# Twenty idle products in place of 130 in the opening of an attention and feed-forward kernel

## The chip, the cores and the metric

The kernel runs on one core of a Trainium2 chip. The metric is the time of one execution on the device in microseconds, as the median of several runs. The profile is of one execution, taken by the hardware profiler; PE is TensorE, PEld its loads of weights, DVE is VectorE, ACT is ScalarE, POOL is GpSimd and SP is SyncE.

## What is computed

Sliding-window causal attention over 8 batches, 8 heads, 576 positions and 64 numbers a head, and a gated feed-forward network on its result:

```python
scores = scale * np.matmul(q, k.transpose(0, 1, 3, 2))
rel = pos[:, None] - pos[None, :]
mask = (rel >= 0) & (rel < 64)
...                                     # softmax over the masked scores
attn_out = np.matmul(attn, v)           # 8 x 8 x 576 x 64
x = attn_out.transpose(0, 2, 1, 3).reshape(4608, 512)
a = x @ w1                              # 512 x 1024
b = x @ w2                              # 512 x 1024
h = a * b @ w3                          # 1024 x 1024
return h @ w_out                        # 1024 x 512
```

Inputs and output are float32.

## The kernel before

Products are made in float16 with sums in float32. Since nothing lies between w3 and w_out, the kernel multiplies these two once, into a 1024 x 512 matrix `wc_sb`, and each token then needs only w1, w2 and `wc_sb`.

Every engine works through its instructions in the order in which the program lists them. The opening (L479 to L642) is an order written out by hand; from there a loop over slots interleaves the attention (18 steps of 256 positions) with the feed-forward part (9 groups of 512 tokens). The change lies in the opening.

What the opening does, for the names that matter here:

- `load_rows` (L419, SP queue) and `load_w3` (L430, POOL queue) bring rows of w3 in blocks of 128; `cast_rows` (L424) turns the blocks that came in float32 into float16. Blocks 0 and 1 come by the first way, blocks 2 and 3 by one transfer of the second way, into the tile that the profile calls `ab`.
- `fold_t(fc)` turns one block by eight products with the identity (L437), into a buffer of the four that are called `f_ps`, and an engine copies the result to `w3T` (L439).
- `load_wo` (L415) brings w_out in two halves of 256 columns, also into a tile called `ab`.
- `fold_mm(fc, c0, c1)` multiplies a turned block by columns of w_out (L444) and copies the result to `wc_sb` (L445).
- `load_qk` (L210) and `load_v` (L230) bring q, k and v; `transposes` (L220, VectorE) makes `kT` and `qT` from them; `scores` (L275) makes 64 small products for one step of attention, `weigh` (L284, L288, L245) the exponentials and the mask, `values` (L301, L307) and `norm` (L317 to L320) the result.
- `ffn_ab` (L367) and `ffn_o` (L383) are the feed-forward products; `store` (L397) writes the output.
- `keep_busy(n)` (L465 to L469) multiplies the identity by itself n times into one buffer of `f_ps` that nothing reads.

TensorE's order in the opening is: eight transposes of block 0, the products of `keep_busy`, sixteen transposes of blocks 2 and 3, the scores of step 0, eight transposes of block 1, and then the folding products of blocks 2, 3, 1 and 0 for the first 256 columns. POOL issues, in this order, the loads of k and q of batch 0, of w3's blocks 2 and 3, makes the band of the mask, and issues the loads of w_out's first and second half, of w3's blocks 4 and 5 and of v.

## Time and profile before

| | |
|---|---|
| median of three runs | 258.71 us (258.62 to 259.79) |
| the profiled execution: its own time | 257.93 us |
| its span | 256.1 us |
| TensorE busy | 245.0 us (96%) |
| VectorE, ScalarE, GpSimd busy | 146.4, 118.9, 114.9 us |
| idle products (L469) | 130, from 5.80 us on |
| first folding product (L444) | 18.46 us |

Times in the profile count from the start of the span; the execution's own time is longer by 1.8 us. In a row of the timeline stand the start, the time from the first start to the last end of the instructions that were merged, the engine, the line and the operation, what is written and read, how many, and in brackets the idle time before and what ended it. In a row of one line's instructions stand the shortest, the median and the longest duration of one in ns, and the first and the last start. A row of the chain has a start, a length and what filled it.

### The profile page before, as it was taken

The page shows a single profiled execution, that of the slowest core. Times are in us where ns is not written, and L with a number is a line of the kernel's source. Part 1 is how long each engine was busy: PE and PEld are TensorE (multiplying, and loading weights), DVE is VectorE, ACT ScalarE, POOL GpSimd, SP SyncE. Part 2 cuts the span into 40 slices and gives each one's busy share as a digit, 9 for nine tenths or more (in the row PEclk, how much of TensorE's full clock was granted, in tenths as well). Part 3 has the DMA queues.
Part 4 walks back from the last instruction along what each step waited for, and adds up shares of the span by engine and source line. Part 5 has one row for each costly group of instructions (what it writes and reads, how often), then busy time and mean ns, then how long its engine had stood idle before and what let it go on. Part 6 is the DMA issues. An engine that isn't in the chain of part 4 may idle for free.

```text
span 256.1 us, 8262 instructions
## 1 busy us (share of the span) xinstructions
PE 245.0 (96%) x3612; PEld 129.6 (51%) x3612; DVE 146.4 (57%) x217; ACT 118.9 (46%) x178; POOL 114.9 (45%) x153
## 2 busy tenths in 40 slices
PE   2989999999999999999999999999999999999991
PEld 2988654454445544445444444454444544444441
DVE  1173936778777646557764774675566345434420
ACT  2143672384475564454526444545465455233210
POOL 8873858599769855881097036003000303003000
PEclk9999999999999999999999999999999999999999
DMA  6999999999996999599079909401300220021022
GB/s 202 198 179 183 205 205 200 155 188 177 195 116 75 179 202 170 80 186 189 7 121 200 129 0 163 99 5 41 127 3 5 84 88 1 3 94 75 1 82 89
DMA packets 75657, 30.09 MB, mean 117 GB/s; under 512 B 62488, under 2 KB 70040, under 8 KB 75616
## 3 DMA queue, kind: packets, MB, share of 16 engines
q0 software_dynamic: 69712, 18.88, 74.0%
q1 hardware_dynamic: 5616, 10.44, 11.0%
q8 instruction: 29, 0.48, 0.8%
q10 hardware_dynamic: 288, 0.20, 0.2%
q14 instruction: 12, 0.10, 0.1%
HBM read 38.80 MB, written 9.44 MB: 188 GB/s over the span
## 4 chain that ended last, share of the span: by engine, by line
PE 90%; DMA 5%; POOL 1%; ACT 1%; issue 0%; DVE 0%; POOLq 0%
PE f_ps L367 49%; PE f_ps L383 24%; PE f_ps L444 6%; PE a_ps L275 4%; PE a_ps L307 4%; DMA ab<-in_moe_w_out_dram 3%; PE a_ps L301 2%; DMA k<-in_k_dram 2%; ACT pt L284 1%; PE f_ps L437 1%; POOL ab L430 0%; POOL band L247 0%; POOL band L245 0%; POOL band L254 0%; DVE t2k L390 0%
## 5 line engine op out<-in xcount | busy, mean ns | idle before, releaser
L367 PE MATMUL f_ps<-xT,w_sb 128*128 128x512 f16 x576 | 129.5, 379 | 0.0
L367 PEld LDWEIGHTS <-w_sb 128*128 128x128 f16 x576 | 54.7, 98 | 64.5 <-issue 0.8
L371 DVE TENSOR_TENSOR ab<-f_ps,a_sb 128x512 f16<-128x512 f32 x72 | 49.6, 690 | 41.0 <-PE f_ps L367 37.6
L383 PE MATMUL f_ps<-wc_sb,ab 128*128 128x512 f16 (+1 forms) x296 | 65.6, 374 | 0.0
L370 ACT COPY a_sb<-f_ps 128x512 f32<-128x512 f32 x72 | 42.2, 587 | 46.2 <-PE f_ps L367 46.2
L245 POOL TENSOR_SCALAR_AFFINE_SELECT pt<-pt 128x1024 f16<-128x1024 f16 x11 | 13.0, 1180 | 79.6 <-ACT pt L284 79.6
L383 PEld LDWEIGHTS <-ab 128*128 128x128 f16 x296 | 27.9, 98 | 31.0
L284 ACT ACTIVATE pt<-a_ps 128x1024 f16<-128x1024 f32 x36 | 36.3, 1026 | 15.1 <-PE a_ps L275 15.1
L320 DVE TENSOR_TENSOR xT<-a_ps,r 128x512 f16<-128x512 f32 x36 | 23.2, 687 | 25.1 <-ACT r L318 25.0
L230 POOL DMA_DIRECT2D v<-in_v_dram x40 | 34.6, 885 | 2.6 <-PE f_ps L367 1.1
L386 ACT COPY t2k<-f_ps 128x512 f32<-128x512 f32 (+1 forms) x19 | 10.9, 575 | 42.2 <-PE f_ps L383 42.2
L288 DVE TENSOR_TENSOR pt<-pt,band 128x1024 f16<-128x1024 f16 x25 | 17.3, 695 | 14.1 <-ACT pt L284 13.9
L210 POOL DMA_DIRECT2D k<-in_k_dram x32 | 20.2, 646 | 5.8 <-DMA v<-in_v_dram 3.5
L210 POOL DMA_DIRECT2D q<-in_q_dram x32 | 20.0, 637 | 4.3 <-DMA v<-in_v_dram 1.8
L220 DVE STREAM_TRANSPOSE kT<-k 128x576 int32<-128x576 int32 x16 | 14.9, 936 | 4.3 <-DMA k<-in_k_dram 4.3
L386 DVE COPY t2k<-f_ps 128x512 f32<-128x512 f32 x17 | 11.7, 688 | 9.1 <-PE f_ps L383 9.1
L220 DVE STREAM_TRANSPOSE qT<-q 128x576 int32<-128x576 int32 x16 | 14.8, 934 | 2.2 <-DMA q<-in_q_dram 2.2
L444 PE MATMUL f_ps<-ab,w3T 128*128 128x256 f16 (+1 forms) x96 | 14.6, 308 | 0.3 <-DMA ab<-in_moe_w_out_dram 0.3
L275 PEld LDWEIGHTS <-kT 32*128 32x128 f16 x1152 | 10.5, 92 | 7.8 <-issue 7.0
L307 PE MATMUL a_ps<-pt,v 128*32 128x64 f16 x1152 | 14.0, 193 | 0.0
L317 ACT ACTIVATE ln_s<-a_ps 128x512 f32<-128x512 f32 x18 | 10.8, 598 | 6.6 <-PE a_ps L301 6.5
L307 PEld LDWEIGHTS <-v 128*32 128x32 f16 x1152 | 13.5, 97 | 0.3
(47 smaller groups left out, 135.0 us busy)
## 6 DMA issues: line engine op xcount, KB each, us to landing
out_dram<-t2k SPq DMA_DIRECT2D x35, 256.0 KB, 4.4
k<-in_k_dram POOLq DMA_DIRECT2D x32, 144.0 KB, 7.6
q<-in_q_dram POOLq DMA_DIRECT2D x32, 144.0 KB, 6.6
v<-in_v_dram POOLq DMA_DIRECT2D x32, 128.0 KB, 5.9
w_sb<-in_moe_w_dram POOLq DMA_DIRECT2D x8, 256.0 KB, 9.8
w_sb<-in_moe_w_dram SPq DMA_DIRECT2D x2, 512.0 KB
ab<-in_moe_w_out_dram POOLq DMA_DIRECT2D x2, 512.0 KB, 9.1
xT<-in_moe_w_dram POOLq DMA_DIRECT2D x2, 512.0 KB, 12.5
```

What stands on the lines that cost most here:

```text
L210: nc.gpsimd.dma_start(out=t16_of(b, which)[32 * j:32 * j + 32].rearrange("p hh (i n) -> p (hh i) n", n=r * D), in_=src[b, 2 * j:2 * j + 2] ...
L220: nc.vector.transpose(dst[b][:, hh].rearrange("q t c -> q (t c)").bitcast(I32).rearrange("q (i p r) -> q i r p", p=32, r=r), t16s[which, b ...
L230: nc.gpsimd.dma_start(out=vh[lo:P, c], in_=v[b, :, s0:s0 + P - lo, :].rearrange("h s d -> s h d"))
L284: nc.scalar.activation(pt, held.pop(d).rearrange("k j (a n) -> k (j a) n", a=2), AF.Exp, bias=-SHIFT, scale=scale)
L307: nc.tensor.matmul(o_ps[jp][32 * h:32 * h + 32, 0, o0:o0 + 64], v16s[b % 3][:, max(0, t - 1), 4 * jp + h, x:D:2], pt[:, h, 64 * i:64 * i + ...
L320: nc.vector.tensor_tensor(xT[:, 2 * jp:2 * jp + 2, x0:x0 + W], o_ps[jp][:, 0].rearrange("p (x n) -> p x n", x=2), r[:, jp].unsqueeze(1).br ...
L367: nc.tensor.matmul(d[:, f * n:f * n + n], w[:, dc, (fc + f) * P:(fc + f + 1) * P], xT[:, dc, x0:x0 + n], start=(dc == 0), stop=(dc == 3), ...
L370: act_cp(a_sb[:, 0:nf * n], a_ps[:, 0:nf * n])
L371: nc.vector.tensor_tensor(ab[:, fc:fc + nf, lo:hi], b_ps[:, 0:nf * n].rearrange("p (f n) -> p f n", f=nf), a_sb[:, 0:nf * n].rearrange("p ...
L383: nc.tensor.matmul(o_ps[:, 0:c1 - c0], ab[:, fc, t * P:t * P + P], wc_sb[:, fc, c0:c1], start=(fc == 0), stop=(fc == 7))
L386: cp(o_sb[:, c0:c1], o_ps[:, 0:c1 - c0])
L444: nc.tensor.matmul(o_ps[:, c0:c1], w3Ts[fc][:, ec, :], wo16[:, ec, c0:c1], start=(ec == 0), stop=(ec == 7))
```

## The change

`keep_busy` is called with 20 in place of 130, at the same place. TensorE gets 110 products, with their loads of weights, fewer in the opening. No other instruction and no order is touched.

```diff
     make_band()
     cast_rows(1, 1, act_cp)
-    keep_busy(130)
+    keep_busy(20)
     load_wo(0, 256)
     fold_t(2, act_cp)
     fold_t(3, act_cp)
```

## The prediction

> **What bounds the kernel now.** I read the page first: the span, the busy times, the two rows of slices for TensorE, and the chain by engine.

> ```profile
> span 256.1 us, 8262 instructions
> PE 245.0 (96%) x3612; PEld 129.6 (51%) x3612; DVE 146.4 (57%) x217; ACT 118.9 (46%) x178; POOL 114.9 (45%) x153
> ...
> PE   2989999999999999999999999999999999999991
> ...
> PEclk9999999999999999999999999999999999999999
> ...
> PE 90%; DMA 5%; POOL 1%; ACT 1%; issue 0%; DVE 0%; POOLq 0%
> ```

> TensorE is busy for 96% of the span and carries 90% of the chain. So what matters is how early its real work begins and how fast it then runs. Second came the same engines cut into stretches, for the share in which TensorE has no slack at all.

> ```profile
> core 0: us, PE busy (x) PEld busy (x) DVE busy (x) ACT busy (x) POOL busy (x), PEclk, DMA share, GB/s
> 0.00:5.00 5.00, 0.03 (x1) 0.03 (x2) 0.52 (x3) 1.28 (x1) 4.03 (x12) 1.00 0.54 204
> 5.00:18.50 13.50, 12.64 (x227) 12.30 (x228) 5.71 (x7) 3.69 (x5) 11.12 (x17) 1.00 1.21 188
> 18.50:251.00 232.50, 232.35 (x3386) 117.27 (x3385) 139.89 (x208) 113.72 (x173) 99.78 (x125) 1.00 0.86 112
> 251.00:256.10 5.10, 0.00 (x0) 0.00 (x0) 0.29 (x1) 0.26 (x1) 0.00 (x0) 1.00 0.27 94
> ```

> From 18.50 to 251.00 us TensorE is busy for 232.35 of 232.50 us: 0.15 us of idle time in all. Whatever delays or slows it after 18.5 us reaches the end in full, because no later wait of its own can swallow it. Third: what it waits for, and the chain around 18 us.

> ```profile
> PE f_ps L437 <- DVE ab L424: 5.0, 1, 5.0
> PE a_ps L275 <- DVE kT L220: 0.5, 1, 0.5
> PE f_ps L444 <- DMA ab<-in_moe_w_out_dram: 0.3, 1, 0.3
> ```

> ```profile
> 10.21 8.21 DMA ab<-in_moe_w_out_dram
> 18.42 0.04 issue
> 18.46 6.27 PE f_ps L444 x56
> ```

> TensorE has only three waits. The last real gate is the first half of w_out, issued at 10.21 us and landed at 18.42, which releases the first folding products (L444) at 18.46. Before that gate TensorE's work is not on the chain, and the 130 idle products (L469) lie wholly there. Fourth, TensorE's timeline up to the gate:

> ```profile
> 4.97 1.03 PE L437 MATMUL f_ps<-ident,ab 128*128 128x128 f16 x8 [4.97 <-DVE ab L424]
> 5.80 9.67 PE L469 MATMUL f_ps<-ident 128*128 128x128 f16 x130
> 15.30 1.06 PE L437 MATMUL f_ps<-ident,ab 128*128 128x128 f16 x16
> 16.88 0.68 PE L275 MATMUL a_ps<-qT,kT 32*128 32x64 f16 x64 [0.52 <-DVE kT L220]
> 17.50 0.62 PE L437 MATMUL f_ps<-ident,ab 128*128 128x128 f16 x8
> 18.46 6.27 PE L444 MATMUL f_ps<-ab,w3T 128*128 128x256 f16 x56 [0.34 <-DMA ab<-in_moe_w_out_dram]
> ```

> The first eight transposes (L437) take 0.83 us from their start to the next group's start, 104 ns each. The sixteen at 15.30 take 1.06 us from first start to last end; less 0.22 us for the last one's own length, that is 15 steps of 56 ns. It is the same operation at nearly double the rate. The line of the idle products, in three windows, shows when it changed:

> ```profile
> L469 PE MATMUL f_ps<-ident x20: 314/314/314, 5.8 to 7.8; 128*128 128x128 f16 x20
> L469 PE MATMUL f_ps<-ident x43: 314/314/314, 5.8 to 10.3; 128*128 128x128 f16 x43
> L469 PE MATMUL f_ps<-ident x83: 219/219/219, 10.6 to 15.2; 128*128 128x128 f16 x83
> ```

> Up to 10.3 us every one lasts 314 ns, from 10.6 us every one 219 ns. I take 10.4 us for the change: 5.4 us after TensorE's first product, 4.6 us after the first idle one. The granted clock reads 1.00 all the way, so that column does not show this; the durations do. The idle products do no work that anything reads. What they leave behind is a TensorE that runs at the fast rate when the gate opens.

> **The change part by part.** *Removed: 110 idle products.* Twenty remain. The first window above is nearly what they will look like: from 5.80, 20 x 104 ns, last end at about 8.1 us. They stop 2.3 us ahead of the moment at which the rate changed, so TensorE falls idle while still slow.

> *What comes earlier: nothing that counts.* The next work is the transposes of w3's blocks 2 and 3. Their rows and the neighbours:

> ```profile
> ab<-in_moe_w_dram POOLq DMA_DIRECT2D x1, 512.0 KB, 7.8
> ```

> ```profile
> 6.99 0.72 POOL L430 DMA_DIRECT2D ab<-in_moe_w_dram  x1 [0.53 <-DMA k<-in_k_dram]
> ...
> 14.00 0.67 DVE L439 COPY w3T<-f_ps 128x1024 f16<-128x1024 f16 x1
> ...
> 15.64 1.18 DVE L220 STREAM_TRANSPOSE kT<-k 128x576 int32<-128x576 int32 x1
> 15.95 1.93 ACT L439 COPY w3T<-f_ps 128x1024 f16<-128x1024 f16 x2 [8.66 <-PE f_ps L437]
> ```

> Issued at 6.99 and landed 7.8 us later, those rows are there at 14.79. So the sixteen transposes start at 14.79 instead of 15.30, and TensorE stands idle for 6.7 us before them. At 104 ns they take 1.66 us, to 16.45 (last end about 16.7), just ahead of the scores' gate, kT's last transpose on VectorE, which ends at 15.64 + 1.18 = 16.82. ScalarE's two copies of them begin at about 15.8 and end near 17.8, where they ended at 17.88 before: no loss. The VectorE queue, the POOL queue with every load, and the order of the four f_ps buffers do not depend on how many idle products are written into their buffer, so kT (16.82) and w_out (18.42) come when they did. The removal itself thus saves 0 us.

> *The slow stretch behind the gates.* I assume the rate is slow when the scores start at 16.88. The scores cost 0.62 us before (16.88 to 17.50). The trace shows none at the slow rate: they cost between 0.62 us (nothing lost) and 0.62 x 104/55 = 1.17 us. I take 1.17, since the transposes right beside them show that ratio. The eight transposes of block 1 follow, 0.83 us instead of 0.45. The folding products then start at 16.88 + 1.17 + 0.83 = 18.88 instead of 18.46: **0.42 us** late, with the 0.34 us wait for w_out used up. (Were the scores not slowed, they would end in time for the gate and this term would be 0.)

> The folding products now run slow until the rate changes. They took 6.27 us for 56, 112 ns each; none is seen slow. By the starts of the 128-column products, each microsecond of slow running loses 1 - 55/104 = 0.47 us; by the recorded durations, 314 against 219 ns, it loses 1 - 219/314 = 0.30 us. I take 0.47, because it is distance between starts that fills a queue without gaps. How long? Before, the change came 5.4 us after the first product. Counted from 16.88, that is 22.3 us: 22.3 - 18.88 = 3.4 us slow, times 0.47 = **1.6 us**. From there the rate is as before.

> *Downstream.* VectorE, ScalarE and the loads only gain margin. With 0.15 us of idle time on TensorE after 18.5 us, nothing takes the delay back. Sum: 0 + 0.42 + 1.6 = **+2.0 us**. The profiled execution took 257.93 us, 1.8 us outside its span of 256.1; with the sum it would be 259.9 (span 258.1). The median of the runs shown is 258.71, 0.8 us above the profiled one; the same 2.0 us on it gives **260.7 us**.

> [...]

> **The rivals.** *Early: the transposes at 14.79 already count.* Between them and the scores TensorE pauses for only about 0.2 to 0.4 us. Counted from 14.79, with 4.6 to 5.4 us, the change comes at 19.4 to 20.2 us; the sum is 0.42 + 0.47 x (0.5 to 1.3) = 0.7 to 1.0 us, so 259.4 to 259.7 us. For it: before, the change came while gaps of this size had not yet occurred, so nothing shows that they reset anything. Against: 1.7 us of work in front of a pause is weak evidence of sustained work.

> *Late: only the dense products count.* If transposes and the small scores (32 rows each) do not speed the engine up, the count starts at 18.88: with 4.6 to 5.4 us, the change comes at 23.5 to 24.3 us and the sum is 0.42 + 0.47 x (4.6 to 5.4) = 2.6 to 3.0 us, so 261.3 to 261.7 us. For it: 4.6 us after the first idle product fits the trace as well as 5.4 after the first transpose. Against: no row separates the two. [...]

> *Not slower: the rate doesn't fall back.* If what changed at 10.4 us depends on the time since TensorE's first product, or if the 2.9 us of work up to 8.1 us are enough, and 6.7 us idle do not undo it, everything from 14.79 on runs at 56 ns. Then the scores start at 16.88, the folding at 18.46, and the time is 258.7 us. It decides at one place: if the folding products stand 112 ns apart from 18.46 on, the sum is 0. For it: the kernel holds the fast rate through its pause of 0.52 us at 16.4. Against: before 10.3 us, 5 us of idle time are followed by slow products, and no row shows a long pause followed by fast ones.

> *Faster: the transfers gain.* Fewer products read memory while w_out is coming in. Were it to land early, the folding could start once block 1's transposes are through, 17.50 + 0.45 = 17.95: at most 0.5 us gained, 258.2 us. Against: the core moved 204 GB/s in the first 5 us with TensorE idle and 188 GB/s with it busy, while the mix of transfers changed too; even the whole gain is below what can be told.

> **How the numbers follow.** A change of 0.5% (1.3 us) is about what a measurement of this kernel can tell from none. Chances: forecast (count from the scores) 0.54, late 0.24, early 0.12, not slower 0.07, faster 0.03. The forecast's own range: with 4.6 us counted from 16.88 and unslowed scores, (21.5 - 18.46) x 0.47 = 1.4 us, so 260.1; at its top 2.0 us, 260.7, with the three runs' spread (258.62 to 259.79) on either side. With the smaller loss of 0.30 per microsecond and unslowed scores it would be 1.2 us, 259.9. The range has to take in late (to 261.7) and early (from 259.4), and a little on top for the spread: 259.4 to 262.0; that leaves out not slower, faster and some tails. Slower by over 0.5%: all of late, nearly all of the forecast (0.02 off for the smaller loss), a sixth of early: 0.78. Within 0.5%: the rest of early, not slower, most of faster: 0.20. Faster by over 0.5%: 0.02.

> **What would show it.** In the profile of the changed kernel: 20 products on L469, all 314 ns, ending near 8.1 us; TensorE idle to about 14.8 us, then transposes of about 314 ns; scores beginning at 16.9 and taking about 1.2 us; folding products (L444, 256 columns) longer than 273 ns at first, with the change near 22.3 us (early: before 20.2; late: after 23.5); from there the same stretches as before, shifted by 2 us, and 0.2 us or less of idle time up to the end. The forecast is wrong if the scores or the folding run at the old durations from the start, if w_out lands at another time than 18.4 us, or if TensorE waits for something new after 19 us that takes the shift back or adds to it.

## The result and the profile after

The changed kernel takes 260.73 us (median of 13 runs, 259.27 to 263.21) where the kernel before took 258.52 us (13 runs beside it): ratio 1.0095, 95% interval 1.0071 to 1.0118. It is slower by 2.2 us by the medians and 2.5 us by the ratio, which is not the quotient of the medians: in the runs below the two differ by up to 0.3%. Forecast were 2.0 us and 260.7 us. The profiled execution took 261.72 us with a span of 260.0 us, so it is one of the slower ones, and its 3.9 us over the span before are more than the typical loss.

The page of the changed kernel, the rows that stand beside those of before:

```profile
span 260.0 us, 8042 instructions
PE 240.6 (93%) x3502; PEld 124.0 (48%) x3502; DVE 146.1 (56%) x217; ACT 118.9 (46%) x178; POOL 113.9 (44%) x153
...
PE   2279999997999999999999999999999999999990
...
PE 91%; DMA 5%; issue 1%; ACT 1%; POOL 0%; DVE 0%; POOLq 0%
```

TensorE's row of slices has its hole in the opening (2 2 7), as the 110 products are gone, but also a 7 in the tenth slice, about 58 to 65 us, where there was a 9. TensorE's waits say what it is:

```profile
PE f_ps L437 <- DMA ab<-in_moe_w_dram: 6.4, 1, 6.4
PE f_ps L437 <- DVE ab L424: 5.1, 1, 5.1
PE f_ps L383 <- issue: 1.8, 1, 1.8
```

The first is the idle time that was forecast, up to w3's rows at 14.58 us. The wait for kT (0.5 us before; 0.2 to 0.4 us were forecast) is gone too. The wait for w_out (0.3 us before) is gone, as forecast. The last is new: 1.8 us in which TensorE waited for nothing that the profile shows, in front of a feed-forward product. Its timeline, first in the opening (with the last of VectorE's transposes of kT, for which the scores wait), then around that place:

```profile
5.89 2.34 PE L469 MATMUL f_ps<-ident 128*128 128x128 f16 x20
14.58 1.89 PE L437 MATMUL f_ps<-ident,ab 128*128 128x128 f16 x16 [6.35 <-DMA ab<-in_moe_w_dram]
15.11 1.18 DVE L220 STREAM_TRANSPOSE kT<-k 128x576 int32<-128x576 int32 x1
16.40 1.04 PE L275 MATMUL a_ps<-qT,kT 32*128 32x64 f16 x64
17.38 1.03 PE L437 MATMUL f_ps<-ident,ab 128*128 128x128 f16 x8
18.20 7.49 PE L444 MATMUL f_ps<-ab,w3T 128*128 128x256 f16 x56
25.53 1.06 PE L437 MATMUL f_ps<-ident,xT 128*128 128x128 f16 x16
...
57.72 0.60 PE L383 MATMUL f_ps<-wc_sb,ab 128*128 128x512 f16 x2
60.13 1.47 PE L383 MATMUL f_ps<-wc_sb,ab 128*128 128x512 f16 x6 [1.81 <-issue]
61.53 0.29 PE L301 MATMUL a_ps<-pt,ones 128*32 128x256 f16 x4
```

The last of these rows stood in the kernel before at:

```profile
58.53 0.29 PE L301 MATMUL a_ps<-pt,ones 128*32 128x256 f16 x4
```

The scores take 0.98 us to the next group's start (0.62 before), block 1's transposes 0.82 us (0.45 before), the 56 folding products 7.33 us (6.11 before, both to the next group's start). Yet the folding starts at 18.20 us, 0.26 us earlier than before (18.46): kT's last transpose ends at 16.29 us here and ended at 16.82, and the folding does not wait for w_out. The pause lies between the second and the third of eight products that add up into one buffer, and no operand or semaphore that the profile shows holds the third up. And the folding products themselves, in two stretches (their durations in ns):

```profile
L444 PE MATMUL f_ps<-ab,w3T x9: 421/421/421, 18.2 to 19.9; 128*128 128x256 f16 x9
L444 PE MATMUL f_ps<-ab,w3T x45: 272/273/337, 20.6 to 25.4; 128*128 128x256 f16 x45
```

They are slow until about 20.5 us, then as before. Against the kernel before, TensorE's instructions are 0.96 us late at 25.53 (24.57 before) and 1.09 us late at 37.81 (36.72); behind the pause it is 3.00 us at 61.53 (58.53), and the last copy of VectorE starts 2.95 us late (254.24, 251.29 before). The rest of the span's 3.9 us lies behind that copy, in the last stores, in this execution. So two things cost time: the opening, with 1 us up to 25.53 us where twice that was forecast, and a pause of 1.8 us, which was not forecast at all.

### The profile page after: what moved, and what is told of

It is laid out like the page before. It is cut to its first block, busy times and chain, and to the rows that moved or that the text cites. A ratio compares the mean times of both kernels' runs of the same rounds, so it can differ in the third digit from the quotient of the medians.

```text
span 260.0 us, 8042 instructions
## 1 busy us (share of the span) xinstructions
PE 240.6 (93%) x3502; PEld 124.0 (48%) x3502; DVE 146.1 (56%) x217; ACT 118.9 (46%) x178; POOL 113.9 (44%) x153
## 3 DMA queue, kind: packets, MB, share of 16 engines
q0 software_dynamic: 69712, 18.88, 71.9%
## 4 chain that ended last, share of the span: by engine, by line
PE 91%; DMA 5%; issue 1%; ACT 1%; POOL 0%; DVE 0%; POOLq 0%
PE f_ps L367 49%; PE f_ps L383 24%; PE f_ps L444 6%; PE a_ps L275 4%; PE a_ps L307 3%; DMA ab<-in_moe_w_dram 3%; PE a_ps L301 2%; DMA k<-in_k_dram 2%; PE f_ps L437 2%; ACT pt L284 1%; DVE t2k L390 0%; POOL ident masks.py:199 0%; ACT t2k L390 0%; POOL ident masks.py:197 0%; PE f_ps L462 0%
## 5 line engine op out<-in xcount | busy, mean ns | idle before, releaser
L383 PE MATMUL f_ps<-wc_sb,ab 128*128 128x512 f16 (+1 forms) x296 | 65.8, 374 | 1.8 <-issue 1.8
L383 PEld LDWEIGHTS <-ab 128*128 128x128 f16 x296 | 27.8, 98 | 33.1 <-issue 2.3
L284 ACT ACTIVATE pt<-a_ps 128x1024 f16<-128x1024 f32 x36 | 36.3, 1025 | 15.1 <-PE a_ps L275 15.1
L230 POOL DMA_DIRECT2D v<-in_v_dram x40 | 34.0, 870 | 4.0 <-PE f_ps L367 1.6
L220 DVE STREAM_TRANSPOSE kT<-k 128x576 int32<-128x576 int32 x16 | 14.8, 932 | 3.8 <-DMA k<-in_k_dram 3.8
L220 DVE STREAM_TRANSPOSE qT<-q 128x576 int32<-128x576 int32 x16 | 14.7, 931 | 2.0 <-DMA q<-in_q_dram 2.0
L444 PE MATMUL f_ps<-ab,w3T 128*128 128x256 f16 (+1 forms) x96 | 15.8, 326 | 0.0
L437 PE MATMUL f_ps<-ident,ab 128*128 128x128 f16 x32 | 4.0, 311 | 11.4 <-DMA ab<-in_moe_w_dram 6.4
L275 PEld LDWEIGHTS <-kT 32*128 32x128 f16 x1152 | 10.8, 94 | 7.3 <-issue 7.0
L307 PE MATMUL a_ps<-pt,v 128*32 128x64 f16 x1152 | 14.0, 193 | 0.0
## 6 DMA issues: line engine op xcount, KB each, us to landing
w_sb<-in_moe_w_dram SPq DMA_DIRECT2D x2, 512.0 KB
ab<-in_moe_w_out_dram POOLq DMA_DIRECT2D x2, 512.0 KB, 8.5
xT<-in_moe_w_dram POOLq DMA_DIRECT2D x2, 512.0 KB, 12.1
```

The costliest lines, as they stand in the source:

```text
L220: nc.vector.transpose(dst[b][:, hh].rearrange("q t c -> q (t c)").bitcast(I32).rearrange("q (i p r) -> q i r p", p=32, r=r), t16s[which, b ...
L230: nc.gpsimd.dma_start(out=vh[lo:P, c], in_=v[b, :, s0:s0 + P - lo, :].rearrange("h s d -> s h d"))
L284: nc.scalar.activation(pt, held.pop(d).rearrange("k j (a n) -> k (j a) n", a=2), AF.Exp, bias=-SHIFT, scale=scale)
L307: nc.tensor.matmul(o_ps[jp][32 * h:32 * h + 32, 0, o0:o0 + 64], v16s[b % 3][:, max(0, t - 1), 4 * jp + h, x:D:2], pt[:, h, 64 * i:64 * i + ...
L383: nc.tensor.matmul(o_ps[:, 0:c1 - c0], ab[:, fc, t * P:t * P + P], wc_sb[:, fc, c0:c1], start=(fc == 0), stop=(fc == 7))
L444: nc.tensor.matmul(o_ps[:, c0:c1], w3Ts[fc][:, ec, :], wo16[:, ec, c0:c1], start=(ec == 0), stop=(ec == 7))
```

## The experiments

Theory A is that of the prediction: the whole loss is the slow stretch. Theory B: the slow stretch is worth about 1 us, and the rest is a wait of TensorE for its own program. The page counts what the program's fetch moves (packets, MB, share), before and after:

```profile
q8 instruction: 29, 0.48, 0.8%
```

```profile
q8 instruction: 28, 0.46, 0.7%
```

In both traces every packet of q8 has 16384 bytes; 29 of them stand against 7224 loads of weights and products on TensorE before, 28 against 7004 after, about 250 each, and the other instruction queue (q14) has 12 packets in both. 110 products fewer (220 instructions, a load of weights and a product each) move every boundary between two packets to another place of the code. The count of TensorE's instructions ahead of each such pause, in all profiles of this case that have one of 0.5 us or more:

```
changed kernel 1473   the same again 1473    148 products 1729   32 wide products 705, 1473
138 products 449      10 late products 1473  w_out early 1729
```

1473 - 705 is 3 x 256, 1473 - 449 is 4 x 256, 1729 - 1473 is 256: every pause is at the same place within 256 instructions. With the 250 above, 256 is taken for the instructions of a packet in what follows.

**The changed kernel again** (no edit).

> The changed kernel once more, for a second profile. Theory A (all of the loss is TensorE's slow stretch behind the gates): ratio to the kernel before about 1.008, in the profile slow durations (314 and 421 ns) until somewhere between 18 and 22 us, no idle time on TensorE after 19 us, and the whole shift against the kernel before explained by the slow stretch. Theory B (the slow stretch costs only about 1 us, the rest is the pause of 1.8 us in the middle of a group of products near 58 us, which comes from where the boundaries of the fetched program now fall): the pause is there again, at the same product, of 1 to 2 us.

260.48 us, ratio 1.0069 (1.0030 to 1.0108). The pause is at the same product, 1.7 us:

```profile
59.85 1.47 PE L383 MATMUL f_ps<-wc_sb,ab 128*128 128x512 f16 x6 [1.71 <-issue]
```

**Slow, with the boundaries of before: 2 products**, run twice. 2 and 130 products are 4 and 260 instructions, 256 apart.

```diff
-    keep_busy(20)
+    keep_busy(2)
```

> 2 idle products. TensorE is idle even longer, so the slow stretch is that of the changed kernel (fast again at 18 to 22 us, about 1 us lost). [...] Theory A: as slow as with 20, ratio about 1.008. Theory B: no pause near 58 us, ratio about 1.004 (1 us).

> 2 idle products once more, with more rounds, for the size of the slow stretch alone (boundaries as with 130): slow until 18 to 21 us, no pause; 0.3 to 1.1 us lost, ratio 1.001 to 1.004. Theory A would have 1.008.

259.19 us, 1.0022 (0.9981 to 1.0062), and 258.85 us, 1.0019 (0.9989 to 1.0050): 18 idle products fewer, and less time lost than with 20. Each alone cannot be told from no change, but both exclude the 1.0095 of the change. No view of the profile gives a pause near 58 us for either, but the trace shows what is left of it. The packet is no earlier: in the first run it lands at 58.84 us, in the changed kernel at 58.60. But with 36 instructions fewer ahead of it, the boundary lies 36 instructions later in the code, among the first small products (L307) behind the place of the pause. In the changed kernel these 36 take TensorE from 60.13 to 61.68 us, so nearly all of the 1.8 us is covered by work. The rest, 0.2 us, stands in both runs behind 1473 instructions. In the first run the group with the boundary takes 0.59 us, the next one 0.43:

```profile
59.89 0.59 PE L307 MATMUL a_ps<-pt,v 128*32 128x64 f16 x32
60.42 0.43 PE L307 MATMUL a_ps<-pt,v 128*32 128x64 f16 x32
```

In the second run, the folding starts at 18.73 us and is slow for a moment only:

```profile
15.11 1.89 PE L437 MATMUL f_ps<-ident,ab 128*128 128x128 f16 x16 [8.79 <-DMA ab<-in_moe_w_dram]
16.93 1.04 PE L275 MATMUL a_ps<-qT,kT 32*128 32x64 f16 x64
17.90 1.03 PE L437 MATMUL f_ps<-ident,ab 128*128 128x128 f16 x8
18.73 6.40 PE L444 MATMUL f_ps<-ab,w3T 128*128 128x256 f16 x56
```

**Fast, with the boundaries of the change: 148 products.**

```diff
-    keep_busy(20)
+    keep_busy(148)
```

> 148 idle products: 296 instructions, 256 more than the 40 of the changed kernel, so the pieces of the program end where they end there, while TensorE stays busy to about 16.3 us and is fast when the gates open. Theory A: as the kernel before, ratio 1.000, the first folding product at about 18.4 us at 273 ns. Theory B: the first folding product as early and as fast as that, but the pause of 1 to 2 us near 57 us is there, ratio about 1.005 to 1.007.

259.89 us, 1.0040 (1.0000 to 1.0079). The folding runs at 273 ns from 18.72 us on, and still the pause is there, at the same product as in the changed kernel, though shorter:

```profile
58.04 1.47 PE L383 MATMUL f_ps<-wc_sb,ab 128*128 128x512 f16 x6 [0.55 <-issue]
```

**Busy time without the number: 32 products of 512 columns**, the identity four times side by side as operand.

```diff
+    def keep_wide(n, moving):
+        d = ps_f.tile([P, GT], FP32, name="f_ps")
+        for _ in range(n):
+            nc.tensor.matmul(d.rearrange("p (a n) -> p a n", a=moving.shape[1]), ident16, moving, start=True, stop=True)
...
-    keep_busy(20)
+    keep_wide(32, ident16[:, :].unsqueeze(1).broadcast_to([P, 4, P]))
```

> 32 idle products of 512 columns in place of 20 of 128 columns: about the time on TensorE of the 130 (slow to about 10 us, then 216 ns each, ending near 15 us), with a quarter of the instructions. If the time for which TensorE is busy sets the rate (theories A and B alike), the folding runs at 273 ns from about 18.4 us on, and the slow stretch costs nothing: ratio 1.000 under A; under B 1.000 or up to 1.007, depending on whether a piece of the program ends at a bad place (visible as idle time on TensorE behind 20 us). If the number of products mattered, the folding would start slow, as with 20.

The folding is fast from its start (18.00 us, 56 products in 6.27 us as before; 7.49 us in the changed kernel). The 32 products ran from 6.0 to about 14.2 us, the 20 narrow ones of the changed kernel from 5.89 to 8.23 us, so busy time counts and not the number. But 260.57 us, 1.0067 (1.0031 to 1.0103): two pauses.

```profile
31.08 0.20 PE L307 MATMUL a_ps<-pt,v 128*32 128x64 f16 x1 [1.78 <-issue]
58.77 0.27 PE L307 MATMUL a_ps<-pt,v 128*32 128x64 f16 x10 [0.65 <-issue]
```

64 instructions instead of 40 put the boundary 24 instructions, 12 products, earlier in the code; the second pause is ten products of L307 and two of L383, 12 products, ahead of the place in the changed kernel.

**Other boundaries: 106 and 138 products**, in two kernels; the edit of the first:

```diff
-    keep_busy(20)
+    keep_busy(106)
```

> 106 idle products: TensorE is busy until about 13 to 14 us, so it is fast when the gates open and the folding starts at 273 ns, as before. But the boundaries of the fetched pieces of 256 instructions now fall so that the piece with the two steps of scores near 50 to 54 us is used up in about 3.2 us (its instructions counted off in the trace of the kernel before; 5.1 us is the least there that made no pause up to 60 us, 3.6 us with 148 products made one of 0.55 us). Theory A (only the clock counts): ratio 1.000. Theory B (program fetch): a pause of 0.5 to 2 us near 53 to 54 us, perhaps smaller ones near 33 and 80 us, ratio 1.003 to 1.010.

> 138 idle products: fast when the gates open, and the boundaries fall where no piece of 256 instructions takes less than 5.0 us. Both theories: no slow stretch behind the gates; theory B: no pause above 0.3 us, ratio 1.000 (within 0.2 %). If it were the number of idle products beyond 130 that costs time, and not where the boundaries fall, it would lie between 130 and 148: about 1.002.

The pause expected with 106 did not come: 258.77 us, 1.0038 (1.0006 to 1.0070), and the profile, of one of the fastest executions (257.58 us), has no pause that is put down to nothing. What lay wrong is the count of time from boundary to boundary: the packet in question started at 49.1 us, during feed-forward products, and had landed at 50.3 us, 3.4 us before it was needed. Why the runs are still slower than before by the ratio (0.1% by the medians) is open. With 138: 259.34 us, 1.0028 (0.9997 to 1.0059), not the 1.000 expected, and not to be told from it either. Its profile is of the slowest of the twelve executions (261.39 us); it shows a pause in the opening, where none above 0.3 us was expected, and what came of it:

```profile
16.87:20.28 3.41, 1.75 (x62) 1.42 (x47) 1.29 (x2) 2.25 (x3) 0.83 (x2) 1.00 1.40 198
20.30:23.60 3.30, 3.30 (x18) 2.38 (x16) 0.42 (x1) 0.37 (x1) 1.01 (x2) 0.50 1.55 189
23.80:30.00 6.20, 6.20 (x124) 5.58 (x122) 3.15 (x7) 3.54 (x5) 2.85 (x4) 1.00 1.61 191
```

(Behind the stretch and its length come the busy times of PE, PEld, DVE, ACT and POOL with their counts, then the granted clock: 1.00, 0.50, 1.00.) TensorE paused 0.67 us at a boundary, then 0.99 us for w_out; it was busy 1.75 of 3.41 us, and the clock read 0.50 in the stretch behind, from 20.30 to 23.60 us.

**Only the time ahead of the gates: 10 wide products on the mask's band**, which is ready at 10.2 us.

```diff
-    keep_busy(20)
+    keep_wide(10, band[:, :, :])
```

> 10 idle products of 512 columns, with the band of the mask as operand, which is finished only at about 10.2 us: TensorE is idle from 6 to 10.2 us, busy from 10.2 to about 14.5 us and goes on with the transposes. Ten products are 20 instructions; boundaries as with 138 products. Clock: if the busy time right ahead of the gates is what counts, TensorE is fast again between 13.6 and 17.1 us, so before the folding begins, and the slow stretch costs 0 to 0.1 us; theory B says no pause: ratio 1.000. If many products or an early start were needed, the folding would start slow and the ratio be about 1.003.

258.44 us, 1.0009 (0.9983 to 1.0035): ten products, the right ones, do what 130 do.

```profile
10.28 4.34 PE L476 MATMUL f_ps<-band,ident 128*128 128x512 f16 x10 [4.29 <-POOL band L257]
14.65 1.07 PE L437 MATMUL f_ps<-ident,ab 128*128 128x128 f16 x16
16.30 0.68 PE L275 MATMUL a_ps<-qT,kT 32*128 32x64 f16 x64 [0.58 <-DVE kT L220]
```

The transposes at 14.65 are fast already (sixteen in 1.07 us, 1.06 before and 1.89 in the changed kernel), 4.37 us after the first of the ten; the 13.6 to 17.1 us of the expectation were the author's estimate. The profile has one pause, of 0.8 us, at the same instruction count as the others, where theory B expected none: the count says where a pause can come, not whether it comes.

**Taking away what holds the packet up: a load of v moved down**, with 20 products.

```diff
     ffn_o(0, 0, act_cp)
-    load_v(2, 6, 7)
...
     ffn_ab(1, 0)
+    load_v(2, 6, 7)
     load_v(2, 0, 2, 4)
```

> 20 idle products, boundaries of the changed kernel, but one load of v of batch 2 (two transfers, issued at 52.2 us) is moved 17 lines down, behind the place of the pause. In the profile of the changed kernel the piece that TensorE lacks starts only at 57.7 us, when these transfers are nearly through. If the piece is held up behind the loads, it now comes 1 to 2 us earlier and the pause of 1.7 to 1.8 us falls below 0.8 us: ratio to the kernel before 1.002 to 1.005 instead of 1.007 to 1.009 (the slow stretch of 0.5 to 1 us stays). If the pause has nothing to do with the loads, it stays at 1.7 us and the ratio at 1.007 to 1.009.

259.72 us, 1.0033 (1.0006 to 1.0060), below the 1.0071 to 1.0118 of the change, though not clear of the 1.0030 to 1.0108 of its repeat. The pause is gone. The transfers show why: in the changed kernel no packet of TensorE's program (q8) starts from 54 to 57.6 us, while the loads on POOL's queue (q0) take 137.7% of the 16 engines' time (packets overlap); it starts at 57.7. With the load moved it starts at 55.1, with q0 at 22.8%. The queues in 54 to 57.6 us of the changed kernel, in 57.6 to 58.7 us of it, and in 55.0 to 56.3 us with the load moved:

```profile
q0 software_dynamic: 1815, 0.48, 137.7%
q1 hardware_dynamic: 74, 0.14, 10.2%
q14 instruction: 1, 0.01, 1.4%
```

```profile
q1 hardware_dynamic: 62, 0.11, 26.2%
q0 software_dynamic: 35, 0.00, 6.0%
q8 instruction: 1, 0.02, 5.3%
```

```profile
q1 hardware_dynamic: 125, 0.23, 46.5%
q0 software_dynamic: 53, 0.05, 22.8%
q8 instruction: 1, 0.02, 5.2%
```

Both pauses of the changed kernel end 1.5 us after the packet has landed (58.60 and 60.13 us in its first profile, 58.41 and 59.85 in the second). The six other pauses listed above end 1.0 to 1.5 us after a packet has landed.

**A better version, and the change in it.** w_out's first half is issued ahead of the band; then also the load of v moved as above, with 130 and with 20 products.

```diff
+    load_wo(0, 256)
     make_band()
     cast_rows(1, 1, act_cp)
     keep_busy(130)
-    load_wo(0, 256)
```

> 130 idle products, and the load of w_out's first half issued ahead of the band of the mask instead of behind it: 2.5 us earlier on its queue. The gate at 18.46 us goes away, and the folding starts when block 1's transposes are through, at about 17.9 to 18.0 us: 0.5 us gained, ratio 0.998, if w3's rows (the transposes' gate) and v do not come later for it. If the transfers only share the same bandwidth in another order, k's last transpose stays the gate and nothing else is gained.

> 130 idle products, w_out's first half issued ahead of the band as in the run before, and the load of v moved down so that the program's pieces come sooner near 57 us. The former alone gave 0.9957; its profile still had a pause of 0.88 us at 59.4 us. With that gone: ratio 0.992 to 0.996, no idle time on TensorE between 19 and 250 us above 0.3 us. If the pause was an exception of that one profile, no further gain: 0.9957 as before.

> The same with 20 idle products: the change of this study in a kernel in which the pause has been taken out. Only the slow stretch is left, 0.5 to 1 us; slower than the version with 130 beside it by 0.2 to 0.4 %, and no pause at 58 us. If 20 products cost more than the slow stretch in another way, the distance is 0.7 to 0.9 %, as between the two kernels of the change.

w_out early: 258.01 us, 0.9957 (0.9928 to 0.9986), faster than both kernels of the change. The gate did not go: in the profile the folding starts at 18.11 us after a wait of 0.55 us for w_out, so 0.35 us earlier than before, and where the rest of the gain lies is not shown. This profile (259.05 us, the slowest of the twelve) has a pause, with the 130 products and the boundaries of before, at the place where it lies with 2 products:

```profile
59.41 0.36 PE L307 MATMUL a_ps<-pt,v 128*32 128x64 f16 x24 [0.88 <-issue]
```

So the boundaries of before are not safe from it either. With v later too: 258.15 us, 0.9968 (0.9935 to 1.0001), no pause, the folding at 17.95 us. That is not better than without, so the 0.88 us were no steady cost of it. With 20 products: 259.12 us, 0.9996 (0.9963 to 1.0029), behind the version with 130 beside it by 1.0 us (0.4%) by the medians and 0.3% by the two ratios: within what the slow stretch was said to cost, and less than half the distance of the change itself. Of the pause its profile has 0.2 us left. It also shows the clock at work in its own column (1.00, 0.66, 0.50, 0.70):

```profile
8.00:11.00 3.00, 0.29 (x3) 0.03 (x1) 1.21 (x1) 0.00 (x0) 2.77 (x5) 1.00 1.20 198
11.00:14.00 3.00, 0.00 (x0) 0.00 (x0) 1.45 (x2) 0.00 (x0) 2.87 (x7) 0.66 1.12 199
14.00:17.00 3.00, 2.18 (x44) 1.99 (x48) 2.40 (x3) 1.11 (x2) 3.00 (x4) 0.50 1.42 193
17.00:20.00 3.00, 3.00 (x73) 2.70 (x62) 1.29 (x2) 2.05 (x3) 1.03 (x2) 0.70 1.41 205
```

By the means of these stretches the clock read 1.00 to about 12.0 us and 0.50 from there to about 18.8 us: it fell in TensorE's idle time (8.29 to 14.82 us) and came back 4.0 us after the transposes had begun. Whether the 20 products had brought the full clock ahead of 12.0 us is not shown: all of them last 314 ns, and no product ran from 8.29 us on.

## Why the prediction was right, and where it was not

- **TensorE idles to w3's rows, and what stands behind the gates runs slow**: right. Twenty products at 314 ns, idle to 14.58 (forecast 14.79), scores 0.98 us (forecast 1.17, from 0.62), transposes 0.82 us (0.83), folding products 0.21 us apart until the rate changes (18.2 to 19.9 us in 8 steps; 0.112 before).
- **The start, 0.42 us late**: it did not come. The term took kT (16.82 us) and w_out (18.42 us) to come when they did before. In the changed kernel kT's last transpose ended at 16.29 us and w_out landed at 18.0 us (10.32 + 7.7), so the folding began 0.26 us early. That is no gain that the removal is shown to make: in the thirteen profiles other than that of before, this transpose ends between 16.2 and 16.8 us, with many idle products as with few.
- **How long the slow stretch lasts**: over-sized. The term counted 5.4 us from the scores and set the end at 22.3 us; by the trace's entries of full clock, from which the granted-clock column is made, it was 20.7 us here and 18.8 to 20.8 us in the five other profiles with 2 or 20 products (56 folding products in 7.49 us here, from the first start to the last end, 6.40 to 7.33 us there, 6.27 before). The folding took 7.33 us instead of 6.11, so 1.22 us were lost where 1.6 were forecast. With the start this makes 0.96 us instead of 2.0 in the profile: about 0.7 us of the difference lie in the start and 0.4 us in the length. In the three comparisons without a pause of 0.5 us or more the loss is 0.19 to 0.33%. The count did not begin with the scores: in the second run with 2 products the full clock is there at 19.0 us (the folding products between 18.7 and 20 us have a median of 273 ns, the longest lasts 394), after transposes and small scores since 15.1 and the folding products of the last 0.2 us. So the transposes count, as the rival "early" has it, and "late" is out; but the changed kernel's own 20.7 us lies between the bounds of "early" (before 20.2 us) and of the forecast (22.3 us). What sets the moment is not shown: full clock came 6.1 us after the transposes had begun in the changed kernel (14.58 to 20.7 us) and 3.9 us after in the second run with 2 products (15.11 to 19.0 us). The prediction took one run's 5.4 us for a fixed count.
- **"Nothing takes the delay back", and nothing adds to it**: the first half held, the second failed, and by the prediction's own sign (a new wait of TensorE after 19 us that adds to the shift) its account was not complete. It read 0.15 us of idle time behind 18.5 us and took the program itself for given. 220 instructions fewer moved the packets' boundaries, and in the changed kernel one falls where 256 instructions are used up fast (in 3.4 us, 54.58 to 57.94 us; the other packets of this trace behind 17 us last 4.6 to 13.0 us), by small products of scores and values, while loads hold up the next packet: 1.7 to 1.8 us. That this is the cause of the pause is shown three ways: it is there without the slow stretch (148 products), shrinks to 0.2 us with it when the boundary lies 1.5 us of work later (2 products), and goes when a load in front of the packet is moved.
- **The number**: that 260.7 was met is luck, by errors that offset each other: 1 us too much for the opening, and a pause of nearly 2 us left out. "Not slower" and "faster" did not come.

What stays open: how much of the changed kernel's loss is the pause in a typical run (its two profiles are only two executions; 0.69 to 0.95% with it less 0.19 to 0.33% without is 0.9 to 2.0 us, an estimate), why 106 products cost 0.4% by the ratio without a pause in the profile, why 148 products have a shorter pause at the same boundary, and what else than the loads decides whether a packet comes late: theory B's expectation of a pause, or of none, was wrong for 106, 138 and the ten late products.

## What to carry to other kernels

Idle products were worth here what they did in the last 4.4 us ahead of the real work (10.28 to 14.65 us): put there, on an operand that became ready at the right time, ten of 512 columns did what 130 of 128 do (ratio 1.0009). When instructions were taken away on an engine that hardly ever waits (220 on TensorE, with 0.15 us of idle time behind 18.5 us), the later boundaries of its fetched program moved and a pause of 1.7 to 1.8 us came; look for idle time put down to nothing in the middle of a group, and compare with a version whose count differs by a multiple of the packet (256 instructions here). A forecast that meets its number can still have the wrong parts: compare the shift at several places of the timeline, not only the ends.
